# Splitting the first x load of a gated attention and SwiGLU kernel, and cutting three weight loads into pieces

## The chip, the cores and the metric

The kernel runs on one core of a Trainium2 chip. The metric is the device time of one execution in microseconds, as the median over several runs. The five engines of the core that appear below are TensorE (matrix multiplies; PE in the profile, with its weight loads as PEld), VectorE (DVE), ScalarE (ACT), GpSimd (POOL) and SyncE (SP), which here issues nearly all DMAs. SPq in a profile row is the DMA queue of SyncE.

## What is computed

The input x has 2048 tokens of 512 bf16 features. Two branches are computed from it and mixed token by token.

```
g = sigmoid((x * gate_w).sum(-1, keepdims=True))
a = linear_attention(x, wqkv) @ wo       # 32 heads of 16
b = (silu(x @ w1) * (x @ w3)) @ w2       # inner width 1376
out = g * a + (1 - g) * b
```

The attention is linear: with phi(t) = max(t, 0) + min(exp(t), 1) + 1e-6, kv is the sum over all tokens of phi(k) times v, z the sum of phi(k), and a token's output is phi(q) kv / (phi(q) z + 1e-6). So kv and z need all tokens before the first output of that branch can be made.

## The kernel before, in words

Tokens are cut into 16 tiles of 128 (t) and four blocks of 512 (tb); the 512 features into four parts of 128 (kc). The program is written out in one order by hand (`manual_schedule`): each engine carries out its instructions in the order in which the code calls them, and waits only on semaphores.

All loads are issued at the top, on SyncE's queue (`dq`), in this order: tiles 0 and 1 of x as one load (L128 to L129, tokens 2p and 2p+1 on partition p, so that each partition gets one run of 2 KB); the four quarters of wq and wk, one per kc (`load_wqk`, L125 to L126, 256 KB each); for tiles 2 to 15 a transposing DMA each (`load_xT`, L123), with the natural x tiles between them (L141); then the narrow remainder weights (L143 to L147), w1 and w3 (L148 to L150, each one load of 1280 KB), wv, wo, w2 (L154, one load of 1280 KB) and w2x. One small load of 8 KB goes on ScalarE's queue (L133). The loads share eight semaphores in turn, so a load waits for the one eight places before it to have landed.

TensorE begins with 13 dummy matmuls on a constant (`warm_step`, L357 to L361). Tiles 0 and 1 of x arrive untransposed, and TensorE transposes them itself, as matmuls with the identity (`transpose_block`, L365): kc 0 to 2 of both tiles, 6 transposes, whose results VectorE and ScalarE copy from PSUM into `xT` (L379 to L382). Then come the first projections, all by `proj_mm` (L183): quarter 0 of the weights for k and q of tile 0 and of tile 1, the two transposes of kc 3 with their copy (L393 to L394), quarter 1 for the same four products, and quarters 2 and 3 for k of both tiles, then for q of both.

After that a loop over the tiles projects q and k (L183), lets ScalarE and VectorE form phi (L196 to L201), and accumulates phi(k) with x in four PSUM banks (`g_step`, L231). Then kv and the matrix M2 that joins it with wo are formed once, and for every block of 512 tokens the SwiGLU hidden layer (`glu_step`, L303 to L315), the outputs of both branches (L475, L492), the mix (L498) and the store (L508) follow. A store of tile 0 or 1 writes to every second row of 256, because of the token order of the first load.

Of the kernel before, what the change touches and what calls it, by code (L numbers as in the profile page):

```python
# [8 lines left out]
ACT = mybir.ActivationFunctionType  # L9
# [7 lines left out]
def kernel(  # L17
# [17 lines left out]
    nc = tc.nc  # L35
    P = nc.NUM_PARTITIONS
# [5 lines left out]
    KC = D // P  # L42
# [4 lines left out]
    FC = F // P  # L47
# [11 lines left out]
    x2d = A_x.flatten_outer_dims()  # L59
    out2d = out.flatten_outer_dims()  # L60
    x_t = x2d.rearrange("(t p) d -> p t d", p=P)
    wqkv_r = A_wqkv.rearrange("(kc d) n -> d kc n", d=P)
    w1_r = B_w1.rearrange("(kc d) f -> d kc f", d=P)
    w3_r = B_w3.rearrange("(kc d) f -> d kc f", d=P)
# [8 lines left out]
    ident = consts.tile([P, P], BF16, name="ident")  # L73
# [6 lines left out]
        out=bmask[:], in_=bmask[:], pattern=[[-Dh, HPC], [0, Dh]], compare_op=ALU.is_ge,  # L80
# [3 lines left out]
        out=bmask[:], in_=bmask[:], pattern=[[Dh, HPC], [0, Dh]], compare_op=ALU.is_ge,  # L84
# [22 lines left out]
    xN = consts.tile([P, NT, D], BF16, name="xN")  # L107
# [6 lines left out]
    w1 = consts.tile([P, KC, F0], BF16, name="w1")  # L114
    w3 = consts.tile([P, KC, F0], BF16, name="w3")
    w2 = consts.tile([P, FC, D], BF16, name="w2")
    xT = consts.tile([P, KC, S], BF16, name="xT")
    act_pre = consts.tile([P, 1], BF16, name="act_pre")
    dq = nc.sync
# [5 lines left out]
    def load_wqk(kc):  # L125
        dq.dma_start(out=wqk[:, kc, :], in_=wqkv_r[:, kc, 0 : 2 * D])  # L126

    x_first = x2d[0 : 2 * P, :].rearrange("(p j) d -> p j d", j=2)  # L128
    dq.dma_start(out=xN[:, 0:2, :], in_=x_first)  # L129
    nc.scalar.activation(out=act_pre[:], in_=warm[:, 0:1], func=ACT.Exp)  # L130

    touch = consts.tile([P, 2, 16], BF16, name="touch")
    nc.scalar.dma_start(out=touch[:], in_=wqkv_r[:, 1:3, 0:16])  # L133
    for kc in range(KC):
        load_wqk(kc)
    natural = {3: (2, 4), 5: (4, 8), 8: (8, 16)}
    for t in range(2, NT):
# [4 lines left out]
    with nc.allow_non_contiguous_dma(reason="gate column"):  # L142
        dq.dma_start(  # L143
            out=wr[:, :, 2 * FR : NR], in_=gate_w.rearrange("(kc d o) -> d kc o", d=P, o=1)
        )
    dq.dma_start(out=wr[:, :, 0:FR], in_=w1_r[:, :, F0:F])
    dq.dma_start(out=wr[:, :, FR : 2 * FR], in_=w3_r[:, :, F0:F])  # L147
    for w, w_r, cuts in ((w1, w1_r, (0, KC)), (w3, w3_r, (0, KC))):  # L148
        for a, b in zip(cuts, cuts[1:]):
            dq.dma_start(out=w[:, a:b, :], in_=w_r[:, a:b, 0:F0])  # L150
    dq.dma_start(out=wv[:], in_=wqkv_r[:, :, 2 * D : 3 * D])
    dq.dma_start(out=wo[:], in_=A_wo.rearrange("(kc d) n -> d kc n", d=P))
    w2_r = B_w2[0:F0, :].rearrange("(fc f) d -> f fc d", f=P)
    dq.dma_start(out=w2[:], in_=w2_r)  # L154
    w2x_r = B_w2[F0:F, :].rearrange("(i r) d -> i (r d)", i=RP)
    dq.dma_start(
        out=w2x[:].rearrange("p r d -> p (r d)"),
        in_=w2x_r[None].to_broadcast([TPB, RP, RG * D]),
# [11 lines left out]
    bank = [psum.tile([P, D], FP32, name=f"bank{i}") for i in range(8)]  # L170
    turn = {"mm": 0, "ab": 0}

    def mm_tile():
        turn["mm"] += 1
        return bank[4 + (turn["mm"] - 1) % 4]
# [6 lines left out]
    def proj_mm(ps, t, w, kc):  # L182
        nc.tensor.matmul(  # L183
            ps[:], lhsT=xT[:, kc, t * P : (t + 1) * P], rhs=w[:, kc, :],
            start=(kc == 0), stop=(kc == KC - 1),
        )
# [170 lines left out]
    def warm_step(n):  # L357
        for _ in range(n):
            nc.tensor.matmul(
                bank[7][:, 0:256], lhsT=warm[:, 0:P], rhs=warm, start=True, stop=True  # L360
            )  # L361

    def transpose_block(t, kc, dst):

        nc.tensor.matmul(  # L365
            dst, lhsT=xN[:, t, kc * P : (kc + 1) * P], rhs=ident[:], start=True, stop=True
        )

    def transpose_kc(kc, ps):
        for t in range(2):  # L370
            transpose_block(t, kc, ps[:, t * P : (t + 1) * P])

    warm_step(13)

    for t in range(2):
        transpose_block(t, 0, bank[t][:, 0:P])
    transpose_kc(1, bank[2])
    transpose_kc(2, bank[3])
    nc.vector.tensor_copy(out=xT[:, 0, 0:P], in_=bank[0][:, 0:P])  # L379
    nc.scalar.activation(out=xT[:, 0, P : 2 * P], in_=bank[1][:, 0:P], func=ACT.Copy)  # L380
    nc.vector.tensor_copy(out=xT[:, 1, 0 : 2 * P], in_=bank[2][:, 0 : 2 * P])
    nc.scalar.activation(out=xT[:, 2, 0 : 2 * P], in_=bank[3][:, 0 : 2 * P], func=ACT.Copy)  # L382
    first = {(t, n): mm_tile() for n, t in (("k", 0), ("k", 1), ("q", 0), ("q", 1))}
    w_of = {"k": wk, "q": wq}

    def first_mm(n, t, kc):
        proj_mm(first[t, n], t, w_of[n], kc)

    for kc in range(2):
        for n, t in (("k", 0), ("q", 0), ("k", 1), ("q", 1)):  # L390
            first_mm(n, t, kc)
        if kc == 0:
            transpose_kc(3, bank[0])  # L393
            nc.vector.tensor_copy(out=xT[:, 3, 0 : 2 * P], in_=bank[0][:, 0 : 2 * P])  # L394
    for kc in range(2, KC):
        for t in range(2):
            first_mm("k", t, kc)
# [103 lines left out]
        )  # L501

    def store(t, o, cs=slice(0, D)):
        if t < 2:
            rows = out2d[0 : 2 * P, :].rearrange("(p j) d -> p j d", j=2)[:, t, :]
        else:
            rows = out2d[t * P : (t + 1) * P, :]
        dq.dma_start(out=rows[:, cs], in_=o[:, cs])  # L508

    def out_first(tb):  # L510

        t = tb * TPB
        b_part(t, bank[0], range(AHEAD))
        rem_out_step(tb, bank, started=(0,))
        keep = [mm_tile() for _ in range(TPB)]
        rem_out_step(tb + 1, keep, ends=True)
        rem_keep(tb + 1, keep)
        b_part(t, bank[0], range(AHEAD, FC))
        aga = a_part(t, mm_tile())
        o = work.tile([P, D], BF16, tag="o", bufs=3, name="o")  # L520
        mix(t, bank[0], aga, o)
        store(t, o)

    def out_step(tb, tt):
        t = tb * TPB + tt
        held = tb % 2 == 0
        if held and tt == 0:
            return out_first(tb)
        aga = a_part(t, mm_tile() if held else ab_tile())
        o = work.tile([P, D], BF16, tag="o", bufs=3, name="o")  # L530
        if t < NT - 1:
            b_ps = bank[tt] if held else ab_tile()
            b_part(t, b_ps, range(FC), started=held)
            mix(t, b_ps, aga, o)
            store(t, o)
            return
        for lo, hi in ((0, 2 * P), (2 * P, 3 * P), (3 * P, D)):
            cs = slice(lo, hi)
            b_ps = ab_tile()
            b_part(t, b_ps, range(FC), cs)  # L540
            mix(t, b_ps, aga, o, cs)
            if lo == 0:
                store(t, o, cs)
        store(t, o, slice(2 * P, D))
# [56 lines left out]
```

## Time and profile before

| | us |
|---|---|
| median of 3 runs (178.05 to 178.58) | 178.08 |
| the profiled execution | 178.0 |
| its span, first to last instruction | 176.3 |
| TensorE busy | 172.5 |
| VectorE busy | 110.4 |
| POOL busy | 63.2 |
| ScalarE busy | 59.1 |
| first quarter of wq/wk issued, last one issued | 1.25, 2.66 |

All figures in rows of the trace are microseconds from the start of the span, or durations; a row of the timeline has the start, the time covered, the engine, the line, the operation, its output and inputs, how many instructions are merged in it, and in brackets how long the engine sat idle before and what ended that. A busy TensorE is not TensorE at its peak: matmuls overlap, and a 512-column one is listed with 379 ns where the next starts 216 ns after it.

### The profile page before, as it was taken

To read this page: it belongs to the slowest core of one execution; us is meant where nothing else is said; L and a number is where in the kernel's file an instruction comes from. 1 tells how busy PE (TensorE), PEld (TensorE's weight loads), DVE (VectorE), ACT (ScalarE), POOL (GpSimd) and SP (SyncE) were. 2 spreads that over 40 slices of the span, in tenths; PEclk is the share of its full clock that TensorE was granted. 3 is DMA by queue.
4 is the path that set the end of the run, shared out by engine and by line. 5 is a ranking of instruction groups with operands and counts; after the bars stand their busy time and mean duration, and the time that the engine had idled before them with its cause. 6 is when DMAs were issued, how large, how long until landed. Compare 5 with 4: busy or idle time off the path is not lost.

```text
span 176.3 us, 2685 instructions
## 1 busy us (share of the span) xinstructions
PE 172.5 (98%) x969; PEld 82.5 (47%) x969; DVE 110.4 (63%) x207; ACT 59.1 (34%) x109; POOL 63.2 (36%) x106
## 2 busy tenths in 40 slices
PE   8999999999999999999999999999999999999993
PEld 5444444444456443444444466444444444444453
DVE  1399788888764899777343477853435775344363
ACT  4354544544753443422423101134225123422000
POOL 5086657557300668486400044550000562000000
DMA  6998959995204111323200013330000233000001
GB/s 186 262 178 228 183 103 279 402 349 198 66 4 52 26 30 34 83 65 89 60 0 0 0 33 84 84 89 0 0 4 0 60 89 89 4 0 0 30 30 60
DMA packets 29232, 15.57 MB, mean 88 GB/s; under 512 B 21028, under 2 KB 27428, under 8 KB 29220
## 3 DMA queue, kind: packets, MB, share of 16 engines
q1 hardware_dynamic: 28948, 15.41, 35.3%
q8 instruction: 7, 0.11, 0.3%
q10 hardware_dynamic: 272, 0.01, 0.1%
q14 instruction: 5, 0.04, 0.1%
HBM read 8.86 MB, written 2.10 MB: 62 GB/s over the span
## 4 chain that ended last, share of the span: by engine, by line
PE 94%; DMA 2%; SPq 1%; DVE 0%; issue 0%
PE bank L492 20%; PE bank L303 20%; PE bank L309 20%; PE bank L183 15%; PE bank L231 8%; PE bank L475 8%; PE bank L245 3%; DMA wqk<-in_A_wqkv_dram 2%; PE bank L278 2%; SPq L126 1%; PE bank L447 0%; SPq L129 0%; PE bank L462 0%; DVE o L498 0%
## 5 line engine op out<-in xcount | busy, mean ns | idle before, releaser
L315 DVE TENSOR_TENSOR hT<-bank,sg 128x512 bf16<-128x512 f32 x40 | 27.3, 682 | 31.0 <-PE bank L309 30.9
L303 PE MATMUL bank<-xT,w 128*128 128x512 bf16 x160 | 41.1, 379 | 0.0
L309 PE MATMUL bank<-xT,w 128*128 128x512 bf16 x160 | 41.1, 379 | 0.0
L314 ACT ACTIVATE sg<-bank 128x512 bf16<-128x512 f32 x40 | 23.9, 597 | 45.9 <-PE bank L303 45.9
L492 PE MATMUL bank<-w,hT 128*128 128x512 bf16 (+2 forms) x180 | 37.5, 355 | 0.0
L337 POOL TENSOR_TENSOR pqs<-pq,rden 128x512 bf16<-128x512 bf16 x16 | 16.9, 1056 | 54.4 <-issue 46.9
L183 PE MATMUL bank<-wqk,xT 128*128 128x512 bf16 x128 | 30.8, 381 | 0.1
L215 POOL TENSOR_TENSOR zacc<-zacc,pk 128x128 f32<-128x128 f32 x56 | 23.3, 446 | 10.4 <-DVE pk L201 10.4
L492 PEld LDWEIGHTS <-hT 128*128 128x128 bf16 x180 | 16.7, 98 | 18.4 <-issue 0.8
L309 PEld LDWEIGHTS <-w 128*128 128x128 bf16 x160 | 15.7, 98 | 18.9
L303 PEld LDWEIGHTS <-w 128*128 128x128 bf16 x160 | 15.5, 98 | 18.2 <-issue 0.2
L498 DVE SCALAR_TENSOR_TENSOR o<-bank,omg_all,aga 128x512 bf16<-128x512 f32 (+2 forms) x18 | 12.5, 692 | 14.6 <-PE bank L492 11.7
L183 PEld LDWEIGHTS <-xT 128*128 128x128 bf16 x128 | 12.4, 98 | 15.2 <-issue 0.7
L322 POOL TENSOR_TENSOR pr<-pq,zb 128x512 f32<-128x512 bf16 x16 | 18.4, 1154 | 0.1
L231 PE MATMUL bank<-pk,xN 128*128 128x512 bf16 x64 | 16.4, 379 | 0.0
L475 PE MATMUL bank<-M,pqT 128*128 128x512 bf16 x64 | 16.1, 379 | 0.0
L196 ACT ACTIVATE eq<-bank 128x512 bf16<-128x512 f32 x16 | 9.4, 597 | 16.0 <-PE bank L183 16.0
L201 DVE SCALAR_TENSOR_TENSOR pk<-bank,emk 128x512 bf16<-128x512 f32 x16 | 11.1, 692 | 1.6
L196 ACT ACTIVATE ek<-bank 128x512 bf16<-128x512 f32 x16 | 9.4, 597 | 6.7 <-PE bank L183 6.7
L201 DVE SCALAR_TENSOR_TENSOR pq<-bank,emq 128x512 bf16<-128x512 f32 x16 | 11.1, 692 | 0.5
L326 DVE TENSOR_REDUCE den<-pr 128x32 f32<-128x512 f32 x16 | 10.8, 676 | 0.0
L231 PEld LDWEIGHTS <-xN 128*128 128x128 bf16 x64 | 6.3, 98 | 7.6
(54 smaller groups left out, 95.7 us busy)
## 6 DMA issues: line engine op xcount, KB each, us to landing
w<-in_B_w_dram SPq DMA_DIRECT2D x3, 1280.0 KB, 10.2
out_dram<-o SPq DMA_DIRECT2D x15, 128.0 KB, 1.9
wqk<-in_A_wqkv_dram SPq DMA_DIRECT2D x4, 256.0 KB, 3.7
xN<-in_A_x_dram SPq DMA_DIRECT2D x1, 1024.0 KB
xN<-in_A_x_dram SPq DMA_DIRECT2D x2, 256.0 KB, 2.8
xN<-in_A_x_dram SPq DMA_DIRECT2D x1, 512.0 KB, 4.7
wv<-in_A_wqkv_dram SPq DMA_DIRECT2D x1, 512.0 KB, 11.2
wo<-in_A_wo_dram SPq DMA_DIRECT2D x1, 512.0 KB, 12.1
```

What stands on the lines that cost most here:

```text
L183: nc.tensor.matmul(ps[:], lhsT=xT[:, kc, t * P : (t + 1) * P], rhs=w[:, kc, :], start=(kc == 0), stop=(kc == KC - 1),)
L196: nc.scalar.activation(out=e[:], in_=ps[:], func=ACT.Exp)
L201: nc.vector.scalar_tensor_tensor(out=dst, in0=ps[:], scalar=0.0, in1=em[:], op0=ALU.max, op1=ALU.add)
L215: nc.gpsimd.tensor_tensor(out=(zaccb if t == NT - 1 else zacc)[:, cs], in0=zacc[:, cs], in1=pk[t][:, cs], op=ALU.add,)
L231: nc.tensor.matmul(bank[kc][:], lhsT=xN[:, t, kc * P : (kc + 1) * P], rhs=pk[t][:], start=(t == 0), stop=(t == NT - 1),)
L303: nc.tensor.matmul(g_ps[:], lhsT=w1[:, kc, fs], rhs=xT[:, kc, tok], start=(kc == 0), stop=(kc == KC - 1),)
L309: nc.tensor.matmul(u_ps[:], lhsT=w3[:, kc, fs], rhs=xT[:, kc, tok], start=(kc == 0), stop=(kc == KC - 1),)
L314: nc.scalar.activation(out=sg[:], in_=g_ps[:], func=ACT.Silu)
L315: nc.vector.tensor_tensor(out=hT[tb][:, fc, :], in0=u_ps[:], in1=sg[:], op=ALU.mult)
L322: nc.gpsimd.tensor_tensor(out=pr[t][:], in0=pq[:, t, :], in1=zb[:], op=ALU.mult)
L475: nc.tensor.matmul(ps[:], lhsT=pqT[:, c, ts], rhs=M2[:, c, :], start=(c == 0), stop=(c == KC - 1),)
L492: nc.tensor.matmul(ps[:, 0 : cs.stop - cs.start], lhsT=hT[tb][:, fc, tt * P : (tt + 1) * P], rhs=w2[:, fc, cs], start=(fc == 0 and not sta ...
```

## The change

The two first x tiles become two loads of 128 KB with the tokens in their natural order, 1 KB per partition. The order of issue on SyncE is x tile 0, quarter 0 of wq/wk, x tile 1, quarters 1 to 3, then as before. w1 and w3 are loaded in four pieces each (one per kc) and w2 in two. That makes eight more DMAs, one of them ahead of quarter 1.

On TensorE the dummies go from 13 to 10. All four transposes of tile 0 come first, into four banks, and their copies alternate between VectorE and ScalarE; then quarter 0 of k and q for tile 0; then the four transposes of tile 1, into the same banks, and their copies; then quarter 0 for tile 1, quarter 1 for all four products, and quarters 2 and 3 as before. The store of tiles 0 and 1 writes contiguous rows like every other.

```diff
-    x_first = x2d[0 : 2 * P, :].rearrange("(p j) d -> p j d", j=2)
-    dq.dma_start(out=xN[:, 0:2, :], in_=x_first)
+    def load_x(t):
+        dq.dma_start(out=xN[:, t, :], in_=x_t[:, t, :])
+
+    load_x(0)
...
-    for kc in range(KC):
+    load_wqk(0)
+    load_x(1)
+    for kc in range(1, KC):
         load_wqk(kc)
...
-    for w, w_r, cuts in ((w1, w1_r, (0, KC)), (w3, w3_r, (0, KC))):
+    for w, w_r, cuts in ((w1, w1_r, range(KC + 1)), (w3, w3_r, range(KC + 1))):
         for a, b in zip(cuts, cuts[1:]):
             dq.dma_start(out=w[:, a:b, :], in_=w_r[:, a:b, 0:F0])
...
-    dq.dma_start(out=w2[:], in_=w2_r)
+    for a, b in ((0, FC // 2), (FC // 2, FC)):
+        dq.dma_start(out=w2[:, a:b, :], in_=w2_r[:, a:b, :])
...
-    warm_step(13)
-
-    for t in range(2):
-        transpose_block(t, 0, bank[t][:, 0:P])
-    transpose_kc(1, bank[2])
-    transpose_kc(2, bank[3])
-    nc.vector.tensor_copy(out=xT[:, 0, 0:P], in_=bank[0][:, 0:P])
-    nc.scalar.activation(out=xT[:, 0, P : 2 * P], in_=bank[1][:, 0:P], func=ACT.Copy)
-    nc.vector.tensor_copy(out=xT[:, 1, 0 : 2 * P], in_=bank[2][:, 0 : 2 * P])
-    nc.scalar.activation(out=xT[:, 2, 0 : 2 * P], in_=bank[3][:, 0 : 2 * P], func=ACT.Copy)
+    def transpose_tile(t):
+
+        ts = slice(t * P, (t + 1) * P)
+        for kc in range(KC):
+            nc.tensor.matmul(
+                bank[kc][:, 0:P], lhsT=xN[:, t, kc * P : (kc + 1) * P], rhs=ident[:],
+                start=True, stop=True,
+            )
+        for kc in range(KC):
+            if kc % 2 == 0:
+                nc.vector.tensor_copy(out=xT[:, kc, ts], in_=bank[kc][:, 0:P])
+            else:
+                nc.scalar.activation(out=xT[:, kc, ts], in_=bank[kc][:, 0:P], func=ACT.Copy)
+
+    warm_step(10)
+    transpose_tile(0)
...
-    for kc in range(2):
-        for n, t in (("k", 0), ("q", 0), ("k", 1), ("q", 1)):
-            first_mm(n, t, kc)
-        if kc == 0:
-            transpose_kc(3, bank[0])
-            nc.vector.tensor_copy(out=xT[:, 3, 0 : 2 * P], in_=bank[0][:, 0 : 2 * P])
+    for n, t in (("k", 0), ("q", 0)):
+        first_mm(n, t, 0)
+    transpose_tile(1)
+    for n, t in (("k", 1), ("q", 1)):
+        first_mm(n, t, 0)
+    for n, t in (("k", 0), ("q", 0), ("k", 1), ("q", 1)):
+        first_mm(n, t, 1)
...
-        if t < 2:
-            rows = out2d[0 : 2 * P, :].rearrange("(p j) d -> p j d", j=2)[:, t, :]
-        else:
-            rows = out2d[t * P : (t + 1) * P, :]
-        dq.dma_start(out=rows[:, cs], in_=o[:, cs])
+        dq.dma_start(out=out2d[t * P : (t + 1) * P, cs], in_=o[:, cs])
```

More of the change, by code (lines that the diff above doesn't have):

```diff
@@ L361, in warm_step @@
             )
[L363 to L369, printed above, removed]
-        for t in range(2):
-            transpose_block(t, kc, ps[:, t * P : (t + 1) * P])
-    warm_step(13)
-    for t in range(2):
-        transpose_block(t, 0, bank[t][:, 0:P])
-    transpose_kc(1, bank[2])
-    transpose_kc(2, bank[3])
-    nc.vector.tensor_copy(out=xT[:, 0, 0:P], in_=bank[0][:, 0:P])
-    nc.scalar.activation(out=xT[:, 0, P : 2 * P], in_=bank[1][:, 0:P], func=ACT.Copy)
-    nc.vector.tensor_copy(out=xT[:, 1, 0 : 2 * P], in_=bank[2][:, 0 : 2 * P])
-    nc.scalar.activation(out=xT[:, 2, 0 : 2 * P], in_=bank[3][:, 0 : 2 * P], func=ACT.Copy)
+    def transpose_tile(t):
[12 more added lines that the diff above has]
+    transpose_tile(0)
     first = {(t, n): mm_tile() for n, t in (("k", 0), ("k", 1), ("q", 0), ("q", 1))}
```

## The prediction

> **What bounds the kernel now.** I read the page's busy shares and its chain first, then the chain of the first 12 us, then the order of time of TensorE, VectorE, ScalarE and the DMA queue of SyncE up to 10 us, then what the DMA moved in single stretches.
>
> ```profile
> span 176.3 us, 2685 instructions
> PE 172.5 (98%) x969; PEld 82.5 (47%) x969; DVE 110.4 (63%) x207; ACT 59.1 (34%) x109; POOL 63.2 (36%) x106
> PE 94%; DMA 2%; SPq 1%; DVE 0%; issue 0%
> ```
>
> TensorE is busy 98% of the span and the chain of work that ended last is 94% TensorE. What is not TensorE lies at the very front:
>
> ```profile
> 0.80 0.39 SPq L129
> 1.25 0.42 SPq L126
> 1.72 0.43 SPq L126
> 2.19 0.43 SPq L126
> 2.66 4.38 DMA wqk<-in_A_wqkv_dram
> 7.08 2.32 PE bank L183 x10
> ```
>
> This is the chain in order of time. SyncE issues the x pair (0.80) and four quarters of wq/wk; the last quarter (issued 2.66) lands 4.38 us later, at 7.04, and from 7.08 TensorE never stops again. Start to start of its later matmuls, the trace has eight steps longer than the operand calls for, each by 0.09 to 0.10 us, at the changes to smaller shapes. So everything after 7.08 is a train of fixed length, and the change is worth what it does to that 7.08.
>
> ```profile
> 2.71 1.06 PE L359 MATMUL bank<-const-bfloat16-1.0 128*128 128x256 bf16 x4
> 3.57 0.84 PE L365 MATMUL bank<-ident,xN 128*128 128x128 bf16 x6
> 4.26 1.26 PE L183 MATMUL bank<-wqk,xT 128*128 128x512 bf16 x4
> 5.36 0.28 PE L365 MATMUL bank<-ident,xN 128*128 128x128 bf16 x2
> 7.08 1.82 PEld L183 LDWEIGHTS <-xT 128*128 128x128 bf16 x9 [0.41 <-issue]
> ```
>
> TensorE before 7.08: dummy matmuls to 3.57, six transposes, four matmuls of quarter 0 from 4.26, two transposes, then quarters 1 and 2. The last line is the wait for quarter 3: the weight load idles 0.41 us, and the matmul steps there (6.577 to 7.082) show 0.29 us that TensorE could have worked. The pitch also tells the clock: a dummy of 256 columns every 0.213 us and a transpose of 128 every 0.107 us, but after about 4.65 a 512-column matmul every 0.216 us and a transpose in 0.056 us: the pace doubles 3.8 us after the first dummy (0.84).
>
> ```profile
> 3.92 0.29 DVE L379 CAST xT<-bank 128x128 bf16<-128x128 f32 x1 [3.92 <-PE bank L365]
> 4.02 0.28 ACT L380 ACTIVATE xT<-bank 128x128 bf16<-128x128 f32 x1 [1.72 <-PE bank L365]
> DMA packets 1446, 1.43 MB, mean 310 GB/s; under 512 B 809, under 2 KB 809, under 8 KB 1446
> ```
>
> The first two are the copies of the first transposes, 0.35 us behind their transpose and 0.29 us long. The third is what the DMA moved from 1.8 to 6.4 us: 310 GB/s without a pause, so the quarters queue behind one another and the bytes ahead of a load, not its issue, set when it lands.
>
> **The change part by part.** The sum is made against the profiled execution: 178.0 us, a span of 176.3 and 1.7 around it; the median of the three runs is 178.08, 0.08 above it.
>
> *x tile 0 alone.* Half the bytes: 131 KB at 310 GB/s is 0.42 us, so it lands at 3.40 - 0.42 = 2.98. Ten dummies end at 2.93 instead of thirteen at 3.57 (3 x 0.213), so neither waits for the other. Four transposes from about 3.1, the VectorE copy from 3.45 to 3.74 (0.35 + 0.29), first matmul at 3.8. Quarter 0 has 0.42 us less ahead of it, 4.12 - 0.42 = 3.70, and fits. The first matmul comes 0.47 us earlier than the 4.265 of now.
>
> *Tile 1 between the first matmuls.* Two matmuls of 0.427 (half pace) run from 3.8 to 4.65. x tile 1 is there (3.70 + 0.42 = 4.12). Its transposes go at 4.65, the copy at 4.65 + 0.33 to 5.27, so quarter 0 of tile 1 starts at 5.33: between the transposes' end (4.9) and 5.33 TensorE has nothing in order that it may do. Now it has none of that wait, because both tiles are transposed together. Then 2 + 4 + 2 matmuls x 0.216 = 1.73 us, and TensorE stands at quarter 3 at 7.06; now it stands there at 6.79. From the first matmul to there it is 3.26 us instead of 2.52 (4.265 to 6.79): the hole is 0.43 of the difference, one more matmul at half pace 0.2, four transposes in place of two 0.1. So the 0.47 us won are spent, and 0.27 more. VectorE copies 4 x 0.29 in place of 0.29 + 2 x 0.42, ScalarE 4 x 0.28 in place of 0.28 + 0.38, and both idle there until 7.49.
>
> *Quarter 3, the gate.* The small load on ScalarE's queue (8 KB, 0.86) stays where it is. The same 256 KB of x and 1 MB of weights lie ahead of and in it. What differs: x goes in rows of 1 KB instead of 2 KB. The nearest rows are the stretch from 7.2 to 8.2 us, mostly 1 KB packets, at 277 GB/s, and 4.8 to 5.6, mostly 2 KB, at 354. 262 KB cost 0.95 and 0.74, so +0.2 us (ends 0 and 0.25). The extra issue on SyncE puts quarters 1 to 3 and every xT transpose 0.47 us later in the queue. For the quarters I take 0: each lands 3.2 to 4.4 us after its issue while the first packet moves 1.05 us after one, so they wait behind data (quarter 3 would be ready at 3.13 + 1.05 = 4.2 and its turn comes at about 5). The ends are 0 and 0.47. Also tile 0's data may end at 2.27 and quarter 0's begin at 1.27 + 1.05 = 2.3, a hole of 0.03. So quarter 3 lands at 7.04 + 0.2 and its matmul goes at 7.28 instead of 7.08.
>
> *The transposes that follow.* xT of tile 2 now lands at 7.56 and is wanted at 8.16. If it moves by the whole 0.47 it lands at 8.03, wanted at 8.36: covered, by 0.3. Tile 3 lands at 8.07 and is wanted at 9.67; later ones and the natural x tiles have over 2 us.
>
> *w1, w3, w2 in pieces.* Seven more issues at 0.55 us (24.89 to 25.44 is one) are 3.9 us of SyncE; it is done at 36.6 now and next wanted at 46.35. Landings: w1 33.4, w3 36.8, w2 43.3; first use 46.4, 47.2, 67.5. Rows, packets and engines are the same, so I cost it at nothing; w1 would have to lose 13 us to show. Stores of tiles 0 and 1 go to other rows in the same 1 KB pieces: nothing.
>
> *Sum.* +0.2 from quarter 3, 0 from the rest: 178.2, and by the median 178.28. I forecast 178.3 us, a difference that lies inside the 0.3% (0.53 us) which a measurement of this kernel can tell from none. This case reaches from 177.8 to 178.6.
>
> **The rivals.**
> *Clock later (slower).* TensorE's pace doubled after 3.8 us of a train without a break. In the new order the train breaks between 3.53 and 3.8 for the copy and quarter 0, and again at 4.9. If a break restarts that count, half pace lasts to 3.8 + 3.8 = 7.6: quarter 0 of tile 1 from 5.33 to 6.18, four of quarter 1 to 7.74, quarter 2 to 8.17, quarter 3 there, 1.09 us late: 179.1. If the second break counts too, half pace holds for all eight matmuls, to 8.75: 179.7. It decides as soon as the faster pace comes after about 5.5. Against it: the break is 0.27 us, under a tenth of the count. In the Trainium skill, "TensorE: Matmul & The Clock Gate", Part 1, the array starts at half rate and is let go after one busy window of about 3.4 us, the windows running freely. The trace agrees on the doubling and with the 4 us it names. By that page a window spoiled by the break would be followed by the next, 4.65 + 3.41 = 8.06, and quarter 3 would go at 8.4: an estimate of 179.4.
>
> *TensorE's own order becomes the gate.* If quarter 0 doesn't land sooner than now (4.12), the matmuls start at 4.16 and everything up to quarter 3 moves by 0.36, to 7.42: 178.35; with the xT of tile 2 late by a stall like that of tile 4 (four of its sixteen parts land 0.75 us behind the others, at 10.1 instead of 9.3) up to 178.9. For it: only 0.2 us are between TensorE's 7.06 and the gate.
>
> *Quarter 3 sooner (faster).* Quarter 2 came 1.36 us behind quarter 1, against 0.84 between the two before. A few 2 KB packets took 0.6 to 1.0 us from 4.12 on, one microsecond behind the issue of the first xT transpose (3.14). If that was the cause and it moves 0.47 later, quarter 3 may land at 6.3. But TensorE is not there before 7.06, with a smaller copy hole 6.7: 177.6 to 178.0.
>
> **How the numbers follow.** The forecast case 0.50 (of it 0.08 slower than the bound), TensorE's own order 0.22 (0.14 slower), clock later 0.20 (all slower), quarter 3 sooner 0.08 (0.04 faster). Together: faster 0.04, within 0.54, slower 0.42. The range goes from 177.8 to 179.5, to hold most of the clock's case; the forecast case has its own range above.
>
> **What would show it.** Right: the first matmul of quarter 0 near 3.8, a hole near 5, quarter 3 still the last DMA in the chain at the front with its matmul at 7.1 to 7.4, the same train behind it, w1 to w2 landed before 46. Wrong: 512-column matmuls at a pitch of 0.427 after 5.5 (clock); no DMA ahead of TensorE in the chain at 7 us (TensorE's order); a break near 8.3 (xT of tile 2); any new break after 46.

## The result and the profile after

The changed kernel takes 179.3 us (median of 7 runs, 178.82 to 180.92) where the kernel before takes 178.39 (7 runs, 178.05 to 178.58): a ratio of 1.0068, 95% interval 1.0043 to 1.0092. It is slower by 0.91 us; 178.3 had been forecast, 178.28 as the sum. The ratio on record is not the quotient of the two medians, which would be 1.0051; so it is with the ratios below. The profiled execution took 178.82 us, as the fastest of the seven did. Ratios leave out single runs of more than 1.5% above the fastest of their kernel: one of e3 and one of the kernel before, no other.

The page of the changed kernel, its span, its busy engines and the shares of its chain:

```profile
span 176.8 us, 2672 instructions
...
PE 171.0 (97%) x949; PEld 81.9 (46%) x966; DVE 110.5 (63%) x208; ACT 59.4 (34%) x111; POOL 63.2 (36%) x106
...
PE 94%; DMA 2%; issue 1%; SPq 1%; DVE 0%
```

The matmuls are still the chain (949 of 966 are recorded here, so TensorE's busy time reads low). The span is 0.5 us longer, and 178.82 - 176.8 leaves 2.0 us around it, where 178.0 - 176.3 left 1.7. So 0.36 us of this pair's 0.82 lie where no instruction of the program is (with one digit more the span is 176.76).

The chain of the changed kernel in order of time, at the front (start, length, what):

```profile
0.80 0.40 SPq L129
...
1.26 0.41 SPq L126
...
1.72 0.43 SPq L129
...
2.19 3.93 DMA wqk<-in_A_wqkv_dram
6.13 0.04 issue
6.17 3.68 PE bank L188 x16
```

It now goes through quarter 1 of wq/wk, issued 2.19 and landed 6.13. Before, quarter 1 had landed at 4.96. From 6.17 the chain is TensorE's own; its steps still show 0.07 us of waiting for quarter 3 (7.243 to 7.530, where a step takes 0.216).

TensorE in order of time from 2.7 to 10.4 us (start, length, instructions, and the idle time ahead of them with what ended it):

```profile
3.03 0.61 PE L372 MATMUL bank<-ident,xN 128*128 128x128 bf16 x4
4.20 0.76 PE L188 MATMUL bank<-wqk,xT 128*128 128x512 bf16 x2 [0.57 <-DMA wqk<-in_A_wqkv_dram]
4.80 0.39 PE L372 MATMUL bank<-ident,xN 128*128 128x128 bf16 x4
5.41 0.60 PE L188 MATMUL bank<-wqk,xT 128*128 128x512 bf16 x2 [0.22 <-DVE xT L378]
6.17 3.68 PE L188 MATMUL bank<-wqk,xT 128*128 128x512 bf16 x16 [0.16 <-DMA wqk<-in_A_wqkv_dram]
```

And from the order of time of all engines over the first 10 us, the weight load that quarter 3 holds up:

```profile
7.53 1.82 PEld L188 LDWEIGHTS <-xT 128*128 128x128 bf16 x9 [0.19 <-issue]
```

Tile 0 is transposed at 3.03, as forecast, and then TensorE stands until quarter 0 is there at 4.16. The hole behind tile 1's transposes is there too (4.97 to 5.41, start to start). Quarter 3's first matmul goes at 7.53 (7.08 before); the train behind it is as long as it was: 176.76 - 7.53 = 169.23 us against 176.30 - 7.08 = 169.22.

What the DMA moved from 1.8 to 6.4 us, the stretch that gave 310 GB/s before:

```profile
DMA packets 1237, 1.28 MB, mean 278 GB/s; under 512 B 507, under 2 KB 763, under 8 KB 1237
```

That is 0.15 MB less than before by 6.4 us, half a microsecond at 310 GB/s, and of the size of quarter 3's delay (landed 7.49 instead of 7.04).

### The profile page after: what moved, and what is told of

It is laid out like the page before. It is cut to its first block, busy times and chain, and to the rows that moved or that the text cites. A ratio compares the mean times of both kernels' runs of the same rounds, so it can differ in the third digit from the quotient of the medians.

```text
span 176.8 us, 2672 instructions
## 1 busy us (share of the span) xinstructions
PE 171.0 (97%) x949; PEld 81.9 (46%) x966; DVE 110.5 (63%) x208; ACT 59.4 (34%) x111; POOL 63.2 (36%) x106
## 4 chain that ended last, share of the span: by engine, by line
PE 94%; DMA 2%; issue 1%; SPq 1%; DVE 0%
PE bank L308 20%; PE bank L494 20%; PE bank L314 19%; PE bank L188 15%; PE bank L236 8%; PE bank L477 8%; PE bank L250 3%; DMA wqk<-in_A_wqkv_dram 2%; PE bank L283 2%; SPq L129 0%; PE bank L449 0%; SPq L126 0%; PE bank L464 0%; DVE o L500 0%
## 5 line engine op out<-in xcount | busy, mean ns | idle before, releaser
L308 PE MATMUL bank<-xT,w 128*128 128x512 bf16 x158 | 40.8, 379 | 0.2
L314 PE MATMUL bank<-xT,w 128*128 128x512 bf16 x156 | 40.4, 379 | 0.1
L494 PE MATMUL bank<-w,hT 128*128 128x512 bf16 (+2 forms) x176 | 37.0, 355 | 0.5 <-issue 0.3
L220 POOL TENSOR_TENSOR zacc<-zacc,pk 128x128 f32<-128x128 f32 x56 | 23.3, 446 | 10.4 <-DVE pk L206 10.4
L477 PE MATMUL bank<-M,pqT 128*128 128x512 bf16 x61 | 15.6, 379 | 0.1
```

What stands on the lines that cost most here:

```text
L220: nc.gpsimd.tensor_tensor(out=(zaccb if t == NT - 1 else zacc)[:, cs], in0=zacc[:, cs], in1=pk[t][:, cs], op=ALU.add,)
L308: nc.tensor.matmul(g_ps[:], lhsT=w1[:, kc, fs], rhs=xT[:, kc, tok], start=(kc == 0), stop=(kc == KC - 1),)
L314: nc.tensor.matmul(u_ps[:], lhsT=w3[:, kc, fs], rhs=xT[:, kc, tok], start=(kc == 0), stop=(kc == KC - 1),)
L477: nc.tensor.matmul(ps[:], lhsT=pqT[:, c, ts], rhs=M2[:, c, :], start=(c == 0), stop=(c == KC - 1),)
L494: nc.tensor.matmul(ps[:, 0 : cs.stop - cs.start], lhsT=hT[tb][:, fc, tt * P : (tt + 1) * P], rhs=w2[:, fc, cs], start=(fc == 0 and not sta ...
```

## The experiments

The seventeen kernels ran in five groups, each with the kernel before beside them on the same chip, another for each group. The medians of these groups for the kernel before were 178.34, 178.31, 178.34, 178.44 and 178.29 (the last two are told together below). "Outside" is the profiled execution's time less its span. "Late" counts the runs of 180.1 us and more.

| kernel | median us | ratio to before, 95% | outside us | late |
|---|---|---|---|---|
| changed | 179.30 | 1.0068 (1.0043 to 1.0092) | 2.06 | 1 of 7 |
| e1_w_whole | 179.45 | 1.0077 (1.0043 to 1.0110) | 2.04 | 3 of 8 |
| e2_w_split_alone | 178.37 | 1.0007 (0.9990 to 1.0023) | 1.71 | 0 of 12 |
| e3_two_loads_first | 178.87 | 1.0025 (1.0007 to 1.0042) | 1.70 | 1 of 12 |
| e4_order_alone | 179.16 | 1.0044 (1.0027 to 1.0061) | 2.04 | 0 of 10 |
| e5_three_more | 178.55 | 1.0017 (0.9998 to 1.0037) | 2.04 | 0 of 12 |
| e6_order_merged | 178.45 | 1.0011 (0.9993 to 1.0029) | 1.71 | 0 of 12 |
| e7_holes_filled | 179.16 | 1.0050 (1.0033 to 1.0068) | 2.04 | 0 of 12 |
| e8_q_in_hole | 179.59 | 1.0082 (1.0046 to 1.0118) | 2.03 | 3 of 7 |
| e9_after_merged | 179.11 | 1.0046 (1.0026 to 1.0066) | 1.70 | 1 of 12 |
| e10_loads_alone | 180.19 | 1.0078 (1.0046 to 1.0111) | 1.71 | 6 of 11 |
| e11_small_rows | 178.65 | 1.0016 (0.9998 to 1.0033) | 1.70 | 0 of 12 |
| e12_q0_on_scalar | 178.09 | 0.9994 (0.9978 to 1.0011) | 1.72 | 0 of 12 |
| e13_merged_filled | 178.67 | 1.0005 (0.9982 to 1.0028) | 1.71 | 0 of 12 |
| e14_q0_on_scalar_14 | 178.42 | 0.9999 (0.9984 to 1.0015) | 1.70 | 0 of 12 |
| e15_one_more | 178.42 | 0.9996 (0.9982 to 1.0011) | 1.85 | 0 of 10 |
| e16_copies_on_vector | 178.31 | 1.0001 (0.9988 to 1.0015) | 1.71 | 0 of 12 |
| e17_no_small_load | 178.46 | 1.0012 (0.9999 to 1.0024) | 1.70 | 0 of 12 |

The kernel before itself had two late runs (180.33, 180.64) in one group of 30, and none in the others of 23 to 34.

### First group: which part of the change

Three theories stood against one another: A, the loads at the front; B, the pieces of w1, w3 and w2; C, TensorE's order.

*The changed kernel with the weights whole* (e1_w_whole):

```diff
-    for w, w_r, cuts in ((w1, w1_r, range(KC + 1)), (w3, w3_r, range(KC + 1))):
+    for w, w_r, cuts in ((w1, w1_r, (0, KC)), (w3, w3_r, (0, KC))):
...
-    for a, b in ((0, FC // 2), (FC // 2, FC)):
-        dq.dma_start(out=w2[:, a:b, :], in_=w2_r[:, a:b, :])
+    dq.dma_start(out=w2[:], in_=w2_r)
```

> The changed kernel with w1, w3 and w2 loaded whole again, as before; x in two loads and TensorE's new order stay. Theory A (the first quarters of wq/wk land later and less steadily because of the new order of loads at the front): as slow as the changed kernel, ratio to before 1.005 to 1.008, quarter 3's matmul at 7.4 to 8.4. Theory B (the seven extra weight loads cost time, for instance outside the span, where the changed kernel showed 2.0 us instead of 1.7): back to 1.000 to 1.003, with 1.7 us outside the span. Theory C (TensorE's order with tile 1's transposes between): as A.

It was as slow as the changed kernel, 1.0077. Its profile happened to fall on one of the late runs (180.99 us), and shows what those are. TensorE from 2.7 to 10.4 us:

```profile
2.93 0.63 PE L371 MATMUL bank<-ident,xN 128*128 128x128 bf16 x4
4.05 1.01 PE L187 MATMUL bank<-wqk,xT 128*128 128x512 bf16 x2 [0.49 <-DMA wqk<-in_A_wqkv_dram]
4.86 0.63 PE L371 MATMUL bank<-ident,xN 128*128 128x128 bf16 x4
5.55 1.03 PE L187 MATMUL bank<-wqk,xT 128*128 128x512 bf16 x2
6.92 3.72 PE L187 MATMUL bank<-wqk,xT 128*128 128x512 bf16 x10 [0.34 <-DMA wqk<-in_A_wqkv_dram]
```

Ten matmuls of 512 columns cover 3.72 us from 6.92. In the changed kernel's profile sixteen cover 3.68. Start to start they are 0.427 us apart here until the one at 9.44; after that 0.216. The pace doubled at 9.8 us instead of about 4.6.

*The pieces alone* (e2_w_split_alone): the reverse of that diff on the kernel before.

> The kernel before with w1, w3 and w2 in pieces, and nothing else. Theory A and theory C: no change, ratio 0.999 to 1.001, quarter 3's matmul at 7.0 to 7.5 as before. Theory B: 1.002 to 1.007, with 2.0 us outside the span.

No change, 1.0007: theory B falls. In its chain, which like that of the kernel before ends the front with quarter 3, the last quarter landed at 7.61, 0.57 later than in the profile of before, with the same loads at the front:

```profile
2.67 4.94 DMA wqk<-in_A_wqkv_dram
7.61 0.04 issue
```

So a landing in a single profile is good to half a microsecond, no better.

*Two natural x loads, both first* (e3_two_loads_first):

```diff
-    x_first = x2d[0 : 2 * P, :].rearrange("(p j) d -> p j d", j=2)
-    dq.dma_start(out=xN[:, 0:2, :], in_=x_first)
+    for t in range(2):
+        dq.dma_start(out=xN[:, t, :], in_=x_t[:, t, :])
```

The tokens are then in their natural order, so here, in e10 and in e11 the stores of tiles 0 and 1 are those of the changed kernel.

> The kernel before with x tiles 0 and 1 as two loads of 1 KB rows, both still ahead of quarter 0; TensorE's order and 13 dummies as before. Theory A in the form that the small rows and the extra load make the front slower: ratio 1.002 to 1.006, quarters 1 to 3 0.2 to 0.5 us later. If only the place of tile 1 between quarter 0 and quarter 1 matters: 0.999 to 1.001. Theory C: 0.999 to 1.001.

Slower, 1.0025: within A's range. But quarter 3 landed at 7.13, as before; what came late was quarter 0 (4.73 instead of 4.12, its issue at 1.72 instead of 1.25), and TensorE stood 0.56 us for it.

*TensorE's order alone* (e4_order_alone): the kernel before with `transpose_tile` and the new order of the first matmuls, and `warm_step(13)`.

> The kernel before, all its loads as they were, 13 dummies, with only TensorE's new order: tile 0 transposed and its quarter 0 multiplied before tile 1 is transposed. Theory C: slower than before by 0.3 to 0.9 us, ratio 1.002 to 1.005, TensorE itself late for quarter 3 (its matmul behind the one before without a wait, at 7.3 to 7.9). Theory A: 1.000 to 1.002, since TensorE would still wait for quarter 3 or be at most 0.3 us late for it.

1.0044, by C's range. But 0.34 us of the 0.82 lay outside the span: 179.17 - 177.13 = 2.04. All three kernels with the new order had that, the three others 1.70. The rest could be the hole, or the pace, which doubled only at about 6.4 in this profile.

### Second group: the time outside the span, and the pace

The new order has two more ScalarE and one more VectorE instruction than the old (eight copies of 128 columns for tiles 0 and 1, where five did). That suggested two runs.

*Three tiny instructions more* (e5_three_more), on the kernel before:

```diff
+    spare = consts.tile([P, 3], BF16, name="spare")
+    for i in range(2):
+        nc.scalar.activation(out=spare[:, i : i + 1], in_=warm[:, 0:1], func=ACT.Copy)
+    nc.vector.tensor_copy(out=spare[:, 2:3], in_=warm[:, 0:1])
```

> The kernel before with two tiny ScalarE copies and one tiny VectorE copy of a scratch column at the start, where both engines idle; as many instructions on these engines as the new order has. The runs so far have 2.04 us between the span and the execution's time with TensorE's new order, and 1.70 us without it. If these 0.34 us come from the number of ScalarE or VectorE instructions: 2.0 us here, ratio to before about 1.002, the span as before. If they come from something else in the new order: 1.7 us, ratio 1.000.

2.04 us outside, with nothing else changed. Two lines of the page of this run, which took 178.81 us (ScalarE had x109 before):

```profile
span 176.8 us, 2671 instructions
...
PE 172.0 (97%) x952; PEld 82.7 (47%) x969; DVE 110.1 (62%) x208; ACT 59.3 (34%) x111; POOL 63.2 (36%) x106
```

The single runs say it more firmly than the one profile, since each has its span on record: outside it lie 2.01 to 2.07 us in all twelve runs of e5 and 1.66 to 1.77 in all thirty of the kernel before beside them, while the median span is 176.5 and 176.6. The ratio, 1.0017, is what 0.34 us would give (1.0019), though its interval just reaches no change.

*The new order with ScalarE's copies merged* (e6_order_merged), on e4:

```diff
+        dst = [bank[0][:, 0:P], bank[1][:, 0:P], bank[2][:, 0:P], bank[1][:, P : 2 * P]]
+        for kc in (0, 1, 3, 2):
...
+        nc.scalar.activation(
+            out=xT[:, 1:4:2, ts], in_=bank[1][:, 0 : 2 * P].rearrange("p (c q) -> p c q", c=2),
+            func=ACT.Copy,
+        )
```

> The kernel before with TensorE's new order, 13 dummies, and ScalarE's two copies per tile merged into one, so that ScalarE has as many copies as before. If the number of ScalarE instructions is the cause of the 0.34 us outside the span: 1.7 us outside, ratio 1.002 to 1.004. If not: 2.04 us and a ratio like that of the order alone, 1.0044. In both cases the front of the span stays late by the hole behind tile 1's transposes (0.4 us).

1.71 us outside with 112 ScalarE instructions and one VectorE instruction more than before: it is ScalarE's number that counts. And what is left of the new order is 0.14 us (1.0011, not told from no change), though the hole is still in the trace: 0.38 us from tile 1's last transpose to its first matmul, start to start, 0.27 more than in an unbroken train. Theory C shrinks to that. From e4 to e6 the loss fell by 0.68 (0.82 to 0.14 above the kernel before), twice the 0.34; the difference is inside what the two intervals leave open.

*The holes filled with dummies* (e7_holes_filled), on the changed kernel:

```diff
     transpose_tile(0)
...
+    warm_step(3)
     for n, t in (("k", 0), ("q", 0)):
         first_mm(n, t, 0)
     transpose_tile(1)
+    warm_step(1)
```

> The changed kernel with three dummies between tile 0's transposes and its first matmul and one behind tile 1's transposes, where TensorE stands idle. Theory of the clock (idle stretches before the full pace is reached can put it off by a whole window, which made single runs of 180.8 to 181.0): no run above 179.9, median 179.0 to 179.4, ratio 1.003 to 1.005. If those runs come from late landings of the quarters instead: one run in five or more at 180.5 or above, ratio 1.005 to 1.009 as in the changed kernel.

No run above 179.59 in twelve; the four kernels that leave the idle stretches open (changed, e1, and e8 and e9 below) had eight late ones in 34. TensorE in this profile from 2.7 to 10.4 us:

```profile
3.38 0.85 PE L364 MATMUL bank<-const-bfloat16-1.0 128*128 128x256 bf16 x3
4.02 1.06 PE L188 MATMUL bank<-wqk,xT 128*128 128x512 bf16 x2
4.87 0.63 PE L372 MATMUL bank<-ident,xN 128*128 128x128 bf16 x4
5.30 0.42 PE L364 MATMUL bank<-const-bfloat16-1.0 128*128 128x256 bf16 x1
5.57 4.36 PE L188 MATMUL bank<-wqk,xT 128*128 128x512 bf16 x18
```

The pace doubled at 5.9, and quarters 1 to 3 landed as late as in the other runs with these loads (5.93, 6.87, 7.57). In all nineteen profiles together, the three that fell on late runs (e1, e8, e10) have the doubling past 9 us, and none of the others has it past 6.9, while quarter 3 landed at 7.82 and 7.96 in two of the three and at up to 7.99 in runs that were not late. So the late runs are the pace, not the landings. The median fell by 0.14 only, which is inside its uncertainty.

*Quarter 0 of q moved into the hole* (e8_q_in_hole), on the changed kernel:

```diff
-    for n, t in (("k", 0), ("q", 0)):
-        first_mm(n, t, 0)
+    first_mm("k", 0, 0)
     transpose_tile(1)
-    for n, t in (("k", 1), ("q", 1)):
+    for n, t in (("q", 0), ("k", 1), ("q", 1)):
         first_mm(n, t, 0)
```

> The changed kernel with quarter 0 of q for tile 0 moved behind tile 1's transposes, so that it runs while the copy of tile 1 is made. Theory that TensorE's own order is the gate: 0.2 to 0.4 us faster than the changed kernel, ratio to before 1.003 to 1.006. Theory that the landings of quarters 1 to 3 are the gate: no change from the changed kernel, 1.006 to 1.009.

No gain, 1.0082, and three late runs of seven; the hole did close (in its profile, again a late run, matmuls follow tile 1's transposes at once), but TensorE then stood before them, for x tile 1, landed at 4.75. The four runs that were not late (178.97 to 179.59) lie where the six of the changed kernel do (178.82 to 179.63), so closing the hole gained nothing there either.

### Third group: the loads

*The changed kernel with ScalarE's copies merged* (e9_after_merged): the edit of e6.

> The changed kernel with ScalarE's two copies per tile merged into one, so that ScalarE has 112 instructions as before instead of 114. If the two instructions carry 0.34 us of the change's loss: 1.70 us outside the span instead of 2.04, median 178.8 to 179.1, ratio 1.003 to 1.006. If not: 2.04 us and 1.006 to 1.008. Single runs of 180 and more (full pace put off) may still come, since the idle stretches stay.

1.70 us outside, ratio 1.0046: as the price outside the span asks. One late run (180.45), since the idle stretches stayed.

*The changed order of loads alone* (e10_loads_alone): tile 0, quarter 0, tile 1, quarters 1 to 3 on the kernel before, whose TensorE transposes both tiles together.

> The kernel before with the changed kernel's order of loads at the front (tile 0, quarter 0, tile 1, quarters 1 to 3) and nothing else; TensorE's order and 13 dummies as before, so its transposes wait for tile 1. Theory of the loads (the split x moves quarters 1 to 3 back by about 0.4 us): ratio 1.002 to 1.005, quarter 3 landed at 7.4 to 7.6, 1.70 us outside the span; TensorE waits from 3.57 to about 4.5 for tile 1, so that single runs of 180 and more can come. Theory that the loads cost nothing and the rest of the loss is TensorE's order: 0.999 to 1.001.

The slowest of all by its median, 180.19 us, with six of eleven runs late. TensorE from 2.7 to 10.4 us:

```profile
3.57 0.31 PE L366 MATMUL bank<-ident,xN 128*128 128x128 bf16 x1
4.71 0.71 PE L366 MATMUL bank<-ident,xN 128*128 128x128 bf16 x5 [0.83 <-DMA xN<-in_A_x_dram]
5.22 1.91 PE L184 MATMUL bank<-wqk,xT 128*128 128x512 bf16 x4
...
7.14 3.50 PE L184 MATMUL bank<-wqk,xT 128*128 128x512 bf16 x11
```

One transpose, then 1.04 us of nothing until tile 1 is there; the pace doubled at 9.1. Its five other runs lie at 178.77 to 179.19, 0.4 to 0.9 above before, as expected of the loads, with quarter 3 landed at 7.96, later than expected.

*Small rows* (e11_small_rows): both tiles in one load, `in_=x_t[:, 0:2, :]`.

> The kernel before with tiles 0 and 1 of x still in one load, but in the natural order, in 256 rows of 1 KB instead of 128 of 2 KB. If the small rows are what makes the front slower (0.2 us by the prediction): ratio 1.001 to 1.002, x landed at 3.5 to 3.6. If it is the extra load and its issue: 0.999 to 1.001.

1.0016, and x landed at 3.53: the size that was forecast for the rows, but the interval reaches from nothing to twice that.

*Quarter 0 on ScalarE's queue* (e12_q0_on_scalar), on the kernel before:

```diff
-    touch = consts.tile([P, 2, 16], BF16, name="touch")
-    nc.scalar.dma_start(out=touch[:], in_=wqkv_r[:, 1:3, 0:16])
-    for kc in range(KC):
+    nc.scalar.dma_start(out=wqk[:, 0, :], in_=wqkv_r[:, 0, 0 : 2 * D])
+    for kc in range(1, KC):
         load_wqk(kc)
```

> The kernel before with quarter 0 of wq/wk issued on ScalarE's queue in the place of the small load there, which is left out; quarters 1 to 3 follow x directly on SyncE, each 0.47 us earlier. If a load at the front lands a fixed time behind its issue: quarter 0 at 3.7 to 3.9 instead of 4.1 to 4.4, quarters 1 to 3 up to 0.4 us sooner, ratio 0.997 to 0.999. If the bytes ahead set it: quarter 0 as before or later, since it shares the engines with x, quarter 3 at 7.0 to 7.6, ratio 0.999 to 1.002.

Quarter 0 landed at 4.35 though issued at 0.86, and x at 4.02 instead of 3.40: so a fixed time behind the issue does not hold, and the bytes that move beside a load count. But quarters 1 to 3 came at 5.02, 5.70 and 6.46, sooner than the theory of the bytes had expected (7.0 to 7.6 for quarter 3). The profile is of its slowest run, 179.07 us, with the pace doubled at 6.9. The median was 178.09, the lowest of all, but 0.9994 is not told from no change.

### Fourth group: do the pieces add up

*Both repairs of the changed kernel* (e13_merged_filled): the edits of e6 and e7 together.

> The changed kernel with both repairs: ScalarE's two copies per tile merged into one, and four dummies in TensorE's idle stretches. If the two causes add up (0.34 us outside the span, and the put-off full pace), what is left is the later landing of quarters 1 to 3 and the new order: ratio 1.002 to 1.004, no run above 179.4, 1.70 us outside. If a further cause is missing: 1.005 or more.

178.67 us, 0.23 above before, and 1.0005 (0.9982 to 1.0028): below the range that was expected. The two repairs take away 0.68 of the 0.91 us, and what is left is not told from nothing.

*Quarter 0 on ScalarE's queue with 14 dummies* (e14_q0_on_scalar_14).

> The kernel before with quarter 0 on ScalarE's queue in the place of the small load, and 14 dummies instead of 13, because x lands later there. If the earlier quarters 1 to 3 (5.0, 5.7 and 6.5 us in that run) are worth something once TensorE stays busy until x is there: ratio 0.997 to 0.999, median 177.9 to 178.1. If TensorE's half pace is the gate in most runs anyway: 0.999 to 1.001.

0.9999: nothing gained. The quarters landed at 4.12, 4.91, 6.54 and 7.28, so even the earlier ones of e12 were not steady.

*One tiny ScalarE instruction more* (e15_one_more): e5 with one ScalarE copy and no VectorE copy.

> The kernel before with one tiny ScalarE copy of a scratch column at the start. Outside the span 1.70 us were seen with 112 ScalarE instructions and 2.04 with 114. If each costs the same: 1.87 us. If it is a step: 1.70 or 2.04. The span as before.

1.85 us outside (1.80 to 1.91 in the ten runs): half way between 1.70 and 2.04. The median does not show 0.15 us, which it could not.

*Fewer ScalarE instructions*: two copies of the first transposes on VectorE (e16_copies_on_vector, 110 ScalarE instructions), and the 8 KB load left out too, whose result nothing reads (e17_no_small_load, 109).

```diff
-    nc.scalar.activation(out=xT[:, 0, P : 2 * P], in_=bank[1][:, 0:P], func=ACT.Copy)
+    nc.vector.tensor_copy(out=xT[:, 0, P : 2 * P], in_=bank[1][:, 0:P])
...
-    nc.scalar.activation(out=xT[:, 2, 0 : 2 * P], in_=bank[3][:, 0 : 2 * P], func=ACT.Copy)
+    nc.vector.tensor_copy(out=xT[:, 2, 0 : 2 * P], in_=bank[3][:, 0 : 2 * P])
```

> The kernel before with the two ScalarE copies of the first transposes moved to VectorE, so that ScalarE has 110 instructions instead of 112. If every ScalarE instruction costs 0.17 us outside the span (112: 1.70, 113: 1.85, 114: 2.04): 1.36 us outside, ratio 0.998, unless VectorE's later copies (0.3 to 0.5 us) hold TensorE up in the span. If the price sets in at 112 only: 1.70 us, ratio 0.999 to 1.002.

> The same without the 8 KB load on ScalarE's queue too, whose result nothing reads: 109 ScalarE instructions. By 0.17 us each: 1.19 us outside the span, ratio 0.997. If a DMA issue is not counted like the others or the load serves something at the front: as the run above, or slower.

1.71 and 1.70 us outside, the same as with 112: the price sets in above 112 and does not go below 1.70. So no version found here beats the kernel before.

## Why the prediction was wrong, step by step

*What it read from the profile of before.* "From 7.08 TensorE never stops again" and "now it stands there at 6.79": both true of that execution, and neither fixed. The pace of TensorE doubled at about 4.8 in it (inside the matmul step from 4.664 to 4.927). In the nineteen profiles it doubled between about 3.7 and 6.9 sixteen times, in kernels that all start their dummies at 0.84, and three times at 9.1 to 10.2. e2, e5 and e15, with TensorE's program of the kernel before, had it at 5.8, 6.4 and 4.8. A matmul of 512 columns takes 0.427 us ahead of it and 0.216 after it, so each microsecond later costs half a microsecond, and from about 5.4 on TensorE is late for quarter 3 already in the kernel before (6.79 + 0.5 x (5.4 - 4.8) = 7.1). In e5 it came to quarter 3 at 7.56, which had landed at 6.68. The medians say so too: the execution profiled took 178.0, and the groups of 23 to 34 runs gave 178.3 to 178.4, spread over 177.5 to 179.1. The sum was made against an execution faster than most, with a doubling about half a microsecond earlier than the middle one of the sixteen (5.2 to 5.4).

*"Both idle there until 7.49."* With that sentence the two more ScalarE copies were costed at nothing. They run beside other work, and yet cost 0.34 us, outside the span: e5 adds it, e6 and e9 take it away. This is the step that is shown to have failed. It is a third of the loss, and no row of the profile shows it but the execution's time beside its span.

*Quarter 3, "+0.2".* This term was too small. Quarter 3 came 0.45 later in the profile (7.49 against 7.04). Over the profiles it is 7.83 on average in the seven kernels with the changed loads and 7.17 in the eight with the old order of loads, +0.66. The ends given were 0.25 for the rows and 0.47 for the issue. The rows are worth less than was taken: at the front of the traces most packets of 1 KB take 46 ns and most of 2 KB 84, so 256 instead of 128 packets are 1.02 us more, an estimate of 0.06 us when shared by the 16 DMA engines that the profile counts. The delay shows behind tile 1 (quarter 1 at 6.19 against 5.48 on average): from 3.8 to 4.2 us the DMA moved 159 to 279 GB/s in the seven, 287 to 384 in the eight. Whether the 0 taken for the issue is the step at fault was not told apart. e3 has the extra issue too, but with both tiles ahead of quarter 0, and its quarter 3 landed at 7.13; in e11, with the small rows alone, it landed at 7.73. These are single profiles, and with the front loads of the kernel before quarter 3 came anywhere between 6.68 and 7.61. e13 has what the loads and the order are worth once the rest is repaired: 0.23 us. That this is near the forecast +0.2 is luck, since the landing moved by two to three times as much and TensorE was often late by itself.

*Quarter 0 "at 3.70".* 4.16 in the profile, 3.95 on average of the seven, against 4.27 with the old loads: the bytes ahead do count, 0.32 of the 0.42.

*The clock rival (0.20).* Right in kind, wrong in form. A break can put off the doubling, but by more than a new count of 3.8 us: to 9.8, 10.2 and 9.1 us, where 7.6 was worked out. And not in each run: 1 of 7 and 3 of 8, each about 1.6 us longer than the others of its kernel. That the breaks are the cause rests on e7 and e13, which fill them and have no late run in 24, against eight in 34 where they stay open, and on e10, with the longest break (1.04 us) and six late runs in eleven. The kernel before had two late runs in one group of 30, so a break makes such runs more frequent and may not be needed for them; of those two there is no trace. That the median, 179.3, lies inside the stated range and near the 179.1 of this rival is luck: the median run is not a late one, and gets its loss from the other terms.

*TensorE's own order (0.22).* The hole, forecast at 0.43 from the end of the transposes to the next matmul, measured 0.38 in the changed kernel's profile and 0.27 in those of e4 and e6, where the transposes ran at the slower pace. In the profile this rival's condition came true (quarter 0 at 4.16, no sooner than the 4.12 of before), and so did its sign, no DMA ahead of TensorE in the chain at 7 us. TensorE was through with quarter 2 at 7.46, where 7.42 was worked out, but luckily: it waited 0.32 us for quarter 1, which the sum doesn't have, and saved 0.26 because the pace doubled after the first matmul of quarter 0. Quarter 3 came last even so, by 0.07. The price of the order is 0.14 us by e6, not told from none.

*Right:* x tile 0 landed at 2.98, to 0.01 us (2.85 to 2.93 in four other profiles with the changed loads); the weights in pieces cost nothing (e2); the train behind quarter 3 kept its length. Tile 2's xT landed at 8.02, where 8.03 was the most that was allowed for; this is luck, for it came half a microsecond behind a late quarter 3, as before (7.56 behind 7.04).

*The sum, as the runs have it.* 0.91 us = 0.34 outside the span (shown by e5, e9 and e6) + 0.23 left when that and the idle stretches are repaired (e13; loads and order, not told from zero) + 0.34 by difference, which is what the idle stretches must cost on top. The spans of the single runs agree on the split: their median is 177.2 us in the changed kernel and 176.6 to 176.8 in the groups of the kernel before, so about two thirds of the loss lie inside the span and a third outside. The last term is argued, not shown: filling the stretches took 0.14 us from the median in e7 and 0.44 from e9 to e13, and each median is good to some 0.2 us. What the 0.34 us outside the span are made of stays open. The only records of the traces out there are DMA packets ahead of the span, marked as instruction loads, and e5 has as many of them as the kernel before (13).

## What to carry to other kernels

Before an edit is costed against a single profile, look at whether something in it varies from run to run: here the time at which TensorE reached its full pace moved by some 3 us, so a gate read from one execution was not the gate of the median. In a kernel like this one, keep TensorE at work without a break from its first dummy until the pace has doubled; a load that lands 0.3 us sooner is not worth an idle stretch ahead of it. And set the execution's time beside the span in every pair of profiles: a cost may lie in neither trace.

## What the runs showed of the hardware

*ScalarE's instructions have a price outside the span.* Counted in the program (the page leaves out the DMA issue and two others, and has 109 for the kernel before): 109, 110 and 112 ScalarE instructions: 1.70 to 1.72 us between span and execution; 113: 1.85; 114: 2.03 to 2.06. No single run with its span on record breaks this: 1.66 to 1.78 with up to 112, 1.80 to 1.91 with 113, 1.99 to 2.10 with 114. Seven more DMAs on SyncE (e2: 1.71), one more VectorE instruction (e6, e9: 1.71, 1.70) and four more matmuls (e13 against e9: 1.71, 1.70) don't move it. All the added instructions stand at the front of the program; another place was not tried. It is seen in this kernel alone, and whether 112 is a number of ScalarE's or of this program's was not tried.

*When TensorE doubles its pace.* Worked out from where the distance of two matmul starts passes from 0.427 us to 0.216 (or, for 128 and 256 columns, from 0.107 and 0.213 to half of that), the doublings of the nineteen profiles lie at about 3.7, 4.5, 4.6, 4.6, 4.8, 4.8, 4.8, 5.2, 5.4, 5.8, 5.9, 6.2, 6.4, 6.4, 6.6 and 6.9 us, and then at 9.1, 9.8 and 10.2; those that fell in a break are good to some 0.3. The first sixteen spread over 3.2 us, and the earliest (e17) came 2.9 us after the first dummy. The Trainium skill, "TensorE: Matmul & The Clock Gate", Part 1, has windows of 3.41 us that run freely, which such a spread agrees with; its half a microsecond about 4 us does not agree. Taking that length, the windows that ended 3.41 us before the three late doublings held 0.97, 1.01 and 1.04 us without a matmul, and the one with most idle time that still passed held 0.87 (the changed kernel's). One profile does not fit a line between these: in e12 the window that ended 3.41 us before the doubling at 6.87 held 0.79 us without a matmul, all of it ahead of the first dummy, and did not pass. So by this estimate the line lies near a quarter of a window, and no closer than that. The windows are inferred from the doublings, not seen.
